# Window attention and feed-forward: probabilities turned by VectorE instead of TensorE, and the order table left out

## Chip, cores and metric

One core of a Trainium2 chip. The engines are TensorE (PE in the profile; PEld is its weight loads), VectorE (DVE), ScalarE (ACT), GpSimd (POOL) and SyncE (SP, which issues most transfers). The metric is the time of one execution in device microseconds, the median of the runs.

## What is computed

Attention of 8 batches and 8 heads (512 local and 32 global positions, 64 dimensions), then a feed-forward over the joined heads. Global queries see all keys; a local query sees the global keys and the local keys at most 32 positions away.

```python
k_all, v_all = concat([k_g, k_l]), concat([v_g, v_l])
out_g = softmax(q_g @ k_all.T / 8) @ v_all
s_ll = where(abs(pos[:, None] - pos[None, :]) <= 32, q_l @ k_l.T / 8, -1e9)
out_l = softmax(concat([q_l @ k_g.T / 8, s_ll])) @ v_all
x = concat([out_g, out_l]) with heads side by side      # (8 * 544, 512)
h = x @ w_in                                            # 512 -> 2048
out = (h - tanh(h)) @ w_out                             # 2048 -> 512
```

## The kernel before

All operands are fp32; the products of the feed-forward are made of three passes with each factor split into a high and a low part (`x_hi`, `x_lo`, `w_in_hi` and so on).

The attention works on pairs of heads, four pairs for each batch. The first two batches use the class `Pair` (pairs 0 to 7), the other six the class `WindowPair` (pairs 8 to 31, L1441). A window pair goes through these steps:

- loads of keys and queries in blocks of 32 rows (L1459), turned on VectorE in 32x32 blocks (L1472, L1475);
- scores of each block of 32 queries against its three neighbouring blocks and the global keys, 128 small matmuls into two PSUM banks (L1497), and scores of the global queries into two more (L1519);
- a softmax: mask and minimum on VectorE (L1597, L1531), exponentials on ScalarE (L1605, L1561), reciprocals on VectorE (L1611, L1612), normalisation on GpSimd (L1619, L1566). The local probabilities lie in `win_probs`, one buffer for all pairs, one half for each head;
- turning the probabilities, so that keys stand on partitions: 16 TensorE transposes with the identity into two PSUM banks (`transposes`, L1632 to L1644), and two copies into `win_kf` (`add_turned`, L1646, by the helper L998) by ScalarE or VectorE;
- the probabilities of the global queries turned by VectorE (L1586);
- values loaded (L1721), two products, one for each half of the positions (`product`, L1655, matmuls at L1677), and their results split into `x_hi` and `x_lo` (L1706, L1710) with the global part added up in `xg`.

The feed-forward of batch b-1 (class `Chunk`, L1785) runs beside the attention of batch b. It has 16 steps: a hidden step of three passes of four 512-column matmuls (L1816), tanh on ScalarE (L1824), a subtraction on VectorE (L1827) that also frees the hidden step's bank, the split into `ghi` and `glo` (L998, and L1833 on GpSimd or VectorE), and three passes of four output matmuls (L1864). The buffers of that split exist twice. Banks 0 to 3 are shared by hidden steps and the attention, banks 4 to 7 hold the output sums. The last batch's feed-forward and that of the global rows form the tail (class `Tail`, L2035).

The order of all instructions comes from a planner (class `Order`, L51), which runs while the kernel is being built. Every operation has an engine (or a choice, as in `either`, L1000, and `subtract`, L1007), a cost, a due time, what it reads, writes and waits for (`r`, `w`, `res`), and the banks that it takes and frees. The planner always takes the operation that can start first; among those that can start within 0.08 us of each other, the one with the smallest due time. Due times have units of their own: `base(i)` grows by 102.2 for each head, hidden steps are 53.6 apart, and `after(us)` of a window pair is `at` plus 8 for each us. `at` is `base(2j) + CFG["win"]`. Several operations of TensorE can be glued into a visit (`add_visit`, L1682): they run one right after the other, and the banks of all of them are taken before the first.

Before it runs, two tables change the operations by their number: `NUDGE` shifts the due time of 2979 operations (58 to 3036), `CHOICE` adds to the delay that 583 of them have on an engine (L2463 to L2470).

Two visits of a window pair j follow from this (L1976): scores with global scores of j; and products of pair j-1 with transposes of j.

Of the kernel before, what the change touches and what calls it, by code (L numbers as in the profile page):

```python
# [16 lines left out]
P = 128  # L17
# [190 lines left out]
def kernel(ctx, tc, q_l, k_l, v_l, q_g, k_g, v_g, w_in, w_out, out):  # L208
# [107 lines left out]
    def bank(shape, j, dt=F32):  # L316
# [6 lines left out]
        elif len(shape) == 4:  # L323
# [4 lines left out]
    CFG = dict(win=-300.0, a_g=0.7314, a_kg=2.7836, a_ph=2.671, a_qs=2.1456, a_w=0.2133, a_wn=0.6018, a_xg=7.3446, d_g=1.3367, d_gl=1.6793,  # L328
# [20 lines left out]
    NUDGE = {58: -82.9303, 59: -189.1326, 60: -114.5462, 61: -87.6488, 62: -87.6488, 63: -92.8616, 64: -66.6432,  # L349
# [1626 lines left out]
    def window_attention(j):  # L1976
        p, last = pairs[j], pairs[j - 1]
        first = last.b < 2
        if first:
            add_window_masks()  # L1980
        if p.jj == 0:
            add_globals(p.b)
# [527 lines left out]
```

## Time and profile before

| | us |
|---|---|
| median of 3 runs | 952.76 (952.22 to 953.66) |
| the profiled execution | 954.22 |
| its span, first to last instruction | 952.4 |
| PE busy in it | 934.4 |
| DVE, ACT, POOL busy | 550.8, 387.7, 321.7 |

The profile is of one execution. A busy time is the union of an engine's instructions, and the share is of the span. The first feed-forward matmul starts at 62.3 us, the first scores of a window pair at 190.33 us; the tail begins at about 819 us.

### The profile page before, as it was taken

The page shows a single profiled execution, that of the slowest core. Times are in us where ns is not written, and L with a number is a line of the kernel's source. Part 1 is how long each engine was busy: PE and PEld are TensorE (multiplying, and loading weights), DVE is VectorE, ACT ScalarE, POOL GpSimd, SP SyncE. Part 2 cuts the span into 40 slices and gives each one's busy share as a digit, 9 for nine tenths or more (in the row PEclk, how much of TensorE's full clock was granted, in tenths as well). Part 3 has the DMA queues.
Part 4 walks back from the last instruction along what each step waited for, and adds up shares of the span by engine and source line. Part 5 has one row for each costly group of instructions (what it writes and reads, how often), then busy time and mean ns, then how long its engine had stood idle before and what let it go on. Part 6 is the DMA issues. An engine that isn't in the chain of part 4 may idle for free.

```text
span 952.4 us, 24784 instructions
## 1 busy us (share of the span) xinstructions
PE 934.4 (98%) x9762; PEld 769.1 (81%) x9762; DVE 550.8 (58%) x1840; ACT 387.7 (41%) x1116; POOL 321.7 (34%) x637
## 2 busy tenths in 40 slices
PE   7889999999999999999999999999999999999998
PEld 5667877788888888888888878888888888899896
DVE  6977876564556464554544554454555345767773
ACT  6865656353424333433423333342233431424232
POOL 4755645642434332323423333321332331020000
PEclk9989999999999999999999999999999999999999
DMA  9655433622534343334424332242334220100001
GB/s 231 174 145 155 125 109 101 128 48 42 89 62 107 59 71 62 84 80 68 69 48 99 67 63 53 55 82 49 62 66 103 40 40 1 45 1 1 1 1 66
DMA packets 243572, 70.29 MB, mean 74 GB/s; under 512 B 228096, under 2 KB 236800, under 8 KB 243456
## 3 DMA queue, kind: packets, MB, share of 16 engines
q1 hardware_dynamic: 242112, 68.19, 33.5%
q8 instruction: 76, 1.25, 0.6%
q10 hardware_dynamic: 1344, 0.52, 0.2%
q14 instruction: 40, 0.33, 0.1%
HBM read 59.77 MB, written 8.91 MB: 72 GB/s over the span
## 4 chain that ended last, share of the span: by engine, by line
PE 94%; DMA 2%; DVE 2%; issue 1%; ACT 1%; POOL 0%; SPq 0%; ACTq 0%; POOLq 0%; DVEq 0%
PE bank L1864 33%; PE bank L1816 32%; PE bank L2191 7%; PE bank L2311 5%; PE bank L1677 5%; PE bank L1497 3%; PE bank L1641 2%; PE bank L1519 1%; PE bank L1368 1%; PE bank L2217 1%; PE bank L1271 1%; DMA first_raw<-in_k_l_dram 1%; PE bank L1291 1%; PE bank L1175 1%; DMA first_q<-in_moe_w_in_dram 1%
## 5 line engine op out<-in xcount | busy, mean ns | idle before, releaser
L1833 POOL TENSOR_TENSOR glo<-t,ghi 128x512 fp32r<-128x512 f32 x83 | 107.8, 1299 | 269.9 <-PE bank L1864 149.3
L1827 DVE TENSOR_TENSOR t<-bank,t 128x512 f32<-128x512 f32 x112 | 77.3, 691 | 189.4 <-ACT t L1824 189.3
L1824 ACT ACTIVATE t<-bank 128x512 f32<-128x512 f32 x112 | 67.0, 599 | 244.9 <-PE bank L1816 224.1
L1864 PE MATMUL bank<-w_out_hi,glo 128*128 128x512 f32 x448 | 126.6, 397 | 0.0
L1864 PE MATMUL bank<-w_out_hi,ghi 128*128 128x512 f32 x448 | 126.3, 396 | 0.0
L1864 PE MATMUL bank<-w_out_lo,ghi 128*128 128x512 f32 x448 | 125.1, 393 | 0.0
L1816 PE MATMUL bank<-x_hi,w_in_hi 128*128 128x512 f32 x448 | 121.1, 393 | 0.0
L1816 PE MATMUL bank<-x_lo,w_in_hi 128*128 128x512 f32 x448 | 120.0, 390 | 0.0
L1816 PE MATMUL bank<-x_hi,w_in_lo 128*128 128x512 f32 x448 | 119.9, 391 | 0.0
L1605 ACT ACTIVATE prob<-prob,st 128x128 f32<-128x128 f32 x192 | 74.8, 391 | 70.4 <-DVE st L1597 69.9
L1816 PEld LDWEIGHTS bank<-x_hi,w_in_hi 128*128 128x128 f32 x448 | 83.6, 189 | 18.4 <-issue 0.6
L1816 PEld LDWEIGHTS bank<-x_lo,w_in_hi 128*128 128x128 f32 x448 | 83.9, 188 | 17.9 <-issue 0.2
L1816 PEld LDWEIGHTS bank<-x_hi,w_in_lo 128*128 128x128 f32 x448 | 83.6, 188 | 18.2 <-issue 0.8
L1864 PEld LDWEIGHTS bank<-w_out_lo,ghi 128*128 128x128 f32 x448 | 83.6, 188 | 18.3 <-issue 0.5
L1864 PEld LDWEIGHTS bank<-w_out_hi,glo 128*128 128x128 f32 x448 | 83.1, 189 | 18.7 <-issue 0.7
L1864 PEld LDWEIGHTS bank<-w_out_hi,ghi 128*128 128x128 f32 x448 | 82.5, 188 | 18.7 <-issue 1.1
L1619 POOL TENSOR_SCALAR prob<-prob,st 128x128 f32<-128x128 f32 x192 | 69.4, 382 | 76.1 <-DVE st L1612 41.7
L998 ACT CAST ghi<-t 128x512 fp32r<-128x512 f32 (+1 forms) x73 | 44.4, 608 | 46.0 <-PE bank L1864 29.0
L1597 DVE CUSTOM_DVE_ANT_0 prob<-bank,wraw 128x128 f32<-128x128 f32 x192 | 44.6, 283 | 30.0 <-PE bank L1497 30.0
L998 ACT COPY keys_first<-bank 128x512 f32<-128x512 f32 (+2 forms) x83 | 37.2, 497 | 47.6 <-PE bank L1641 33.3
L1677 PEld LDWEIGHTS bank<-keys_first,values 128*64 128x64 f32 x672 | 42.1, 138 | 8.5 <-issue 5.3
L1677 PE MATMUL bank<-keys_first,values 128*64 128x32 f32 (+2 forms) x672 | 46.7, 228 | 0.0
(258 smaller groups left out, 1526.2 us busy)
## 6 DMA issues: line engine op xcount, KB each, us to landing
values<-in_v_l_dram SPq DMA_DIRECT2D x24, 336.0 KB, 4.0
keys_first<-in_v_l_dram SPq DMA_DIRECT2D x24, 336.0 KB, 5.2
out_dram<-wpair SPq DMA_DIRECT2D x28, 256.0 KB, 2.4
rawkq<-in_q_l_dram SPq DMA_DIRECT2D x96, 64.0 KB, 2.3
rawkq<-in_k_l_dram SPq DMA_DIRECT2D x96, 64.0 KB, 2.3
first_q<-in_moe_w_in_dram SPq DMA_DIRECT2D x6, 512.0 KB, 4.5
stage<-in_moe_w_out_dram SPq DMA_DIRECT2D x6, 512.0 KB, 4.4
wpair<-in_moe_w_out_dram SPq DMA_DIRECT2D x6, 512.0 KB, 4.5
```

The costliest lines, as they stand in the source:

```text
L998: (nc.scalar.copy if e == "A" else nc.vector.tensor_copy)(dst, src)
L1597: nc.vector.tensor_tensor_reduce(out=self.prob[h][:, c], in0=self.box["s"][h][:, c], in1=win_mask(t), scale=-0.125, scalar=1e30, op0=ALU.a ...
L1605: nc.scalar.activation(x, x, AF.Exp, bias=s[:, k:k + 1], scale=-1.0, accum_out=s[:, 8 + k:9 + k])
L1619: nc.gpsimd.tensor_scalar(x, x, s[:, k:k + 1], 1.0, op0=ALU.mult, op1=ALU.mult)
L1677: nc.tensor.matmul(dst, win_values[h][:, window(b)], src, start=n == 0, stop=n == len(parts) - 1, skip_group_check=True)
L1816: nc.tensor.matmul(self.h[s][:, j * n:(j + 1) * n], w[:, cc, f * P:(f + 1) * P], self.x()[xi][:, cc, :n], start=part == 0 and cc == 0 and ...
L1824: nc.scalar.activation(tt_[q], self.h[s], AF.Tanh)
L1827: nc.vector.tensor_sub(tt_[q], self.h.pop(s), tt_[q])
L1833: eng[e].tensor_sub(gg[q][1], tt_[q], f32(gg[q][0]))
L1864: nc.tensor.matmul(self.acc[tt], g[:, j * self.n + tt * P:j * self.n + (tt + 1) * P], low_out(f) if wi else high_out(f), start=s == 0 and ...
L2191: nc.tensor.matmul(self.hold(tt, tags), g(), low_out(f) if wi else high_out(f), start=first and k < len(tts), stop=last and k == len(mms) - 1)
L2311: nc.tensor.matmul(dst[:, at], w, m, start=fresh and n == 1, stop=n == 6, skip_group_check=True)
```

## The change

In the window batches the 16 TensorE transposes of a pair and the two copies out of PSUM are gone. Instead `add_turns` issues 16 turns on VectorE from `win_probs` into `win_kf`, eight operations of two instructions. Each instruction takes 32 partitions (block row i of the queries) with 2 heads x 4 tiles x 32 columns and writes 32 partitions (block k of the keys). The products wait for all of them.

The visits are cut otherwise: the global scores of pair j alone; then the products of j with the scores of pair j+1. The next pair's loads are added before that visit. The results of a product are due 18 and not 36 after `at`, and `win` goes from -300 to -100, by which everything in a window pair is due 200 units later. `NUDGE` and `CHOICE` are empty, for all operations, those of the first two batches and of the tail included.

```diff
-    CFG = dict(win=-300.0, a_g=0.7314, a_kg=2.7836, a_ph=2.671, a_qs=2.1456, a_w=0.2133, a_wn=0.6018, a_xg=7.3446, d_g=1.3367, d_gl=1.6793,
+    CFG = dict(win=-100.0, a_g=0.7314, a_kg=2.7836, a_ph=2.671, a_qs=2.1456, a_w=0.2133, a_wn=0.6018, a_xg=7.3446, d_g=1.3367, d_gl=1.6793,
...
-    NUDGE = {58: -82.9303, 59: -189.1326, 60: -114.5462, 61: -87.6488, 62: -87.6488, 63: -92.8616, 64: -66.6432,
...
-    CHOICE = {58: {"A": 7.329, "D": -0.1536}, 76: {"D": -0.24362, "A": -0.2133}, 77: {"D": -0.6068},
...
+    NUDGE = {}
+
+    CHOICE = {}
...
-        def transposes(self):
...
-                            nc.tensor.transpose(box[x][:, h, t], self.prob[h][r, t * P:t * P + P], idn[r, r])
...
-        def add_turned(self):
-            def store(x):
+        def add_turns(self):
+            def turn(k, half):
                 def fn(e, _):
-                    copy(e, view(win_kf, [(CH, 2), (P, NT), (1, 64)], 3 * G + 64 * x), self.box["t"][x])
-                return fn
-
-            for x in range(2):
-                add(either(512, "tp", True), store(x), self.after(9.0), r=[("t", self.j, x)], w=[f"h{x}"], free=[(("t", self.j, x), 1)])
+                    for i in (2 * half, 2 * half + 1):
+                        src = view(win_probs[W * i:W * i + W], [(S, 2), (P, NT), (1, W)], W * k)
+                        nc.vector.transpose(view(win_kf[W * k:W * k + W], [(CH, 2), (P, NT), (1, W)], 3 * G + W * i), src)
+                return fn
+
+            r = [self.p(h, tp) for h in range(2) for tp in range(2)]
+            for k in range(4):
+                for half in range(2):
+                    add(("D", 0.85), turn(k, half), self.after(9.0), r=r, w=[f"hb{k}{half}"], res=self.over)
...
-            return dict(fn=mm, d=0.9, names=[o], r=["h0", "h1", "hg0", "hg1", "vh"], res=[k + (0,) for k in x], rows=1.0, ldw=0.053,
+            return dict(fn=mm, d=0.9, names=[o], r=[f"hb{k}{n}" for k in range(4) for n in range(2)] + ["hg0", "hg1", "vh"], res=[k + (0,) for k in x], rows=1.0, ldw=0.053,
...
-            due = self.after(36.0)
+            due = self.after(18.0)
...
     def window_attention(j):
-        p, last = pairs[j], pairs[j - 1]
-        first = last.b < 2
-        if first:
+        p, other = pairs[j], pairs[j + 1] if j + 1 < len(pairs) else None
+        if j == H:
             add_window_masks()
-        if p.jj == 0:
             add_globals(p.b)
-        p.add_load()
-        p.add_visit(p.at, [p.scores(), p.global_scores()])
+            p.add_load()
+            p.add_visit(p.at, [p.scores()])
+        p.add_visit(p.after(1.0), [p.global_scores()])
         p.add_softmaxes()
         p.add_global_softmax()
-        p.add_visit(p.after(9.0), ([] if first else [last.product(0), last.product(1)]) + [p.transposes()])
-        if not first:
-            last.add_outputs()
-        p.add_turned()
         p.add_values()
         for h in range(2):
             p.add_global_transpose(h)
+        p.add_turns()
+        if other:
+            if other.jj == 0:
+                add_globals(other.b)
+            other.add_load()
+        p.add_visit(p.after(16.0), [p.product(0), p.product(1)] + ([other.scores()] if other else []))
+        p.add_outputs()
...
-    p = pairs[-1]
-    p.add_visit(p.after(32.0), [p.product(0), p.product(1)])
-    p.add_outputs()
```

## Rows read from the trace of the kernel before

**Rows 1.** The page's span and its busy times: us, share of the span, instructions.
```profile
span 952.4 us, 24784 instructions
...
PE 934.4 (98%) x9762; PEld 769.1 (81%) x9762; DVE 550.8 (58%) x1840; ACT 387.7 (41%) x1116; POOL 321.7 (34%) x637
```

**Rows 2.** The page's chain that ended last, by engine.
```profile
PE 94%; DMA 2%; DVE 2%; issue 1%; ACT 1%; POOL 0%; SPq 0%; ACTq 0%; POOLq 0%; DVEq 0%
```

**Rows 3.** Windows of four stages: stretch, length, busy times, PE's granted clock, DMA.
```profile
0.00:60.00 60.00, 47.95 (x485) 35.55 (x487) 46.33 (x188) 45.29 (x146) 31.86 (x65) 0.94 0.74 185
60.00:190.00 130.00, 130.00 (x822) 101.96 (x819) 93.67 (x255) 71.83 (x178) 74.21 (x112) 1.00 0.48 127
190.00:815.00 625.00, 623.27 (x7801) 513.43 (x7800) 320.17 (x1231) 222.72 (x705) 205.78 (x451) 1.00 0.34 64
815.00:952.40 137.40, 133.18 (x661) 118.22 (x659) 90.61 (x169) 47.85 (x90) 9.80 (x10) 1.00 0.05 20
```

**Rows 4.** Timeline of PE, a visit of products and transposes: start, duration, line, form.
```profile
261.01 1.07 PE L1864 MATMUL bank<-w_out_lo,ghi 128*128 128x512 f32 x4
261.92 1.07 PE L1864 MATMUL bank<-w_out_hi,glo 128*128 128x512 f32 x4
262.92 0.30 PE L1677 MATMUL bank<-keys_first,values 128*64 128x96 f32 x1
...
264.62 0.25 PE L1677 MATMUL bank<-keys_first 128*64 128x96 f32 x1
264.80 0.71 PE L1641 MATMUL bank<-idr,prob 64*128 64x64 f32 x16
265.44 1.19 PE L1816 MATMUL bank<-x_hi,w_in_hi 128*128 128x512 f32 x4
```

**Rows 5.** Line L1641, the transposes: durations, first and last start.
```profile
L1641 PE MATMUL bank<-idr,prob x384: 221/222/278, 200.5 to 779.4; 64*128 64x64 f32 x192
```

**Rows 6.** Groups by form, VectorE's turns: count, busy us, mean ns, idle before.
```profile
L1475 DVE STREAM_TRANSPOSE hi<-rawkq 128x512 f32<-128x512 f32 x24 | 16.9, 703 | 7.6 <-PE bank L1497 7.5
...
L1586 DVE STREAM_TRANSPOSE keys_first<-pg 128x192 f32<-128x192 f32 x48 | 16.2, 362 | 14.9 <-PE bank L1677 11.0 <-POOL pg L1566 3.2 <-POOL glo L1833 0.5
```

**Rows 7.** Timeline of VectorE, a turn and the instruction behind it.
```profile
195.07 0.71 DVE L1472 STREAM_TRANSPOSE first_m<-rawkq 128x512 f32<-128x512 f32 x1
195.70 0.32 DVE L1531 CUSTOM_DVE_ANT_0 pg<-bank,wraw 128x192 f32<-128x192 f32 x1
```

**Rows 8.** Groups by form, evictions into keys_first (win_kf's tile) on ScalarE.
```profile
L998 ACT COPY keys_first<-bank 128x512 f32<-128x512 f32 x61 | 33.7, 590 | 45.8 <-PE bank L1641 33.3 <-PE bank L1291 9.5 <-DVE st L1557 2.8
```

**Rows 9.** Timelines of PE and GpSimd, the first window pair.
```profile
190.33 1.43 PE L1497 MATMUL bank<-first_m,hi 64*32 64x64 f32 x124
...
195.21 1.42 POOL L1619 TENSOR_SCALAR prob<-prob,st 128x128 f32<-128x128 f32 x4 [0.41 <-DVE st L1612]
...
197.40 1.43 POOL L1619 TENSOR_SCALAR prob<-prob,st 128x128 f32<-128x128 f32 x4
```

**Rows 10.** The page's transfers: issues, KB each, median us to landing.
```profile
values<-in_v_l_dram SPq DMA_DIRECT2D x24, 336.0 KB, 4.0
keys_first<-in_v_l_dram SPq DMA_DIRECT2D x24, 336.0 KB, 5.2
```

**Rows 11.** Timeline of PE, a visit of scores and what follows it.
```profile
661.54 1.43 PE L1497 MATMUL bank<-first_m,hi 64*32 64x64 f32 x124
...
663.35 1.20 PE L1864 MATMUL bank<-w_out_hi,glo 128*128 128x512 f32 x4
...
666.21 1.07 PE L1816 MATMUL bank<-x_hi,w_in_hi 128*128 128x512 f32 x4
```

**Rows 12.** Timeline of VectorE behind that visit, first and fourth of eight.
```profile
663.06 0.29 DVE L1597 CUSTOM_DVE_ANT_0 prob<-bank,wraw 128x128 f32<-128x128 f32 x1 [1.84 <-PE bank L1497]
...
663.70 0.29 DVE L1597 CUSTOM_DVE_ANT_0 prob<-bank,wraw 128x128 f32<-128x128 f32 x1
```

**Rows 13.** Windows, a stretch of lower clock; columns as in rows 3.
```profile
47.80:54.60 6.80, 4.65 (x23) 2.58 (x25) 5.25 (x20) 4.93 (x13) 3.82 (x6) 0.50 0.54 143
```

More of the change, by code (lines that the diff above doesn't have):

```diff
@@ L1630, in add_softmaxes @@
                     add(("P", 0.77), norm(h, tp), due(3.5 + 2.0 * h), r=[("inv", self.u, h)], w=[self.p(h, tp)])
-        def transposes(self):
-            names = [("t", self.j, x) for x in range(2)]
-            def mm(e, tags):
-                box = self.box["t"] = [bank([P, 2, NT, 64], tags[n]) for n in names]
-                for h in range(2):
-                    for t in range(NT):
-                        for x in range(2):
-                            r = slice(64 * x, 64 * x + 64)
-                            nc.tensor.transpose(box[x][:, h, t], self.prob[h][r, t * P:t * P + P], idn[r, r])
-            return dict(fn=mm, d=0.57, names=names, r=[self.p(h, tp) for h in range(2) for tp in range(2)] + ["idr"], res=["h0", "h1"] + self.over,
-                        rows=0.7, ldw=0.053, tail=0.053, mode="r")
-        def add_turned(self):
-            def store(x):
+        def add_turns(self):
+            def turn(k, half):
                 def fn(e, _):
-                    copy(e, view(win_kf, [(CH, 2), (P, NT), (1, 64)], 3 * G + 64 * x), self.box["t"][x])
-                return fn
-            for x in range(2):
-                add(either(512, "tp", True), store(x), self.after(9.0), r=[("t", self.j, x)], w=[f"h{x}"], free=[(("t", self.j, x), 1)])
+                    for i in (2 * half, 2 * half + 1):
+                        src = view(win_probs[W * i:W * i + W], [(S, 2), (P, NT), (1, W)], W * k)
+                        nc.vector.transpose(view(win_kf[W * k:W * k + W], [(CH, 2), (P, NT), (1, W)], 3 * G + W * i), src)
+                return fn
+            r = [self.p(h, tp) for h in range(2) for tp in range(2)]
+            for k in range(4):
+                for half in range(2):
+                    add(("D", 0.85), turn(k, half), self.after(9.0), r=r, w=[f"hb{k}{half}"], res=self.over)
         def product(self, half):
@@ L2047, in __init__ @@
             self.acc = {}
-            self.was = ["raw", "kq", "ww", "hk0", "gm", "h0", "h1", "vh", ("gkq", 0), ("gkq", 1), "pg00", "pg01", "pg10", "pg11", "pw00", "pw01", "pw10", "pw11", "pg0", "pg1", "pl0", "pl1", "p00", "p10",
+            self.was = ["raw", "kq", "ww", "hk0", "gm", *[f"hb{k}{n}" for k in range(4) for n in range(2)], "vh", ("gkq", 0), ("gkq", 1), "pg00", "pg01", "pg10", "pg11", "pw00", "pw01", "pw10", "pw11", "pg0", "pg1", "pl0", "pl1", "p00", "p10",
                         "p01", "p11", "h00", "h01", "h10", "h11", "hg0", "hg1", "vh0", "vh1", "ga", "gb", ("wraw", 2)]
```

630 rows, old and new, of tables (CHOICE, NUDGE) are left out of this document.

## Prediction

> **What bounds the kernel now.** I read the page's head first: PE is busy 934.4 of 952.4 us, and the chain that ended last is PE for 94% [rows 1, 2]. Then the stages: PE lacks 12.0 us before 60 us, nothing from 60 to 190, 1.7 us from 190 to 815 and 4.2 us after that [rows 3]. A matmul that is merely late by a tenth would still look busy there, so I went to the timeline of PE: groups of four 512-column matmuls follow each other at 0.91 us, and the next visit of the attention begins as soon as the last has been fed in [rows 4]. So between 60 and 815 us the kernel is as long as the list of its matmuls. Two things follow. Work taken off PE there shortens the kernel by its full length. And nothing in the order can be improved there: a new order can only put idle time in, or leave it as it is.
>
> **What leaves PE.** In the window batches a pair's probabilities are turned by 16 transposes [rows 5], 24 pairs. One such set stands on PE from 264.80 us, and the next feed-forward matmul starts at 265.44 us [rows 4]: 0.64 us. A little of the switch may go too: from the last product, at 264.62 us, to the first transpose there are 0.18 us, against 0.09 us from the feed-forward (its last group is through at 261.92 + 0.91 us) to the first product at 262.92 us [rows 4]; that is at most 0.10 us more. 24 x 0.64 = **15.4 us** off the path; the bounds are 15.4 and 24 x 0.74 = 17.8 us. I take 15.4, because another kind of work (the scores) takes the place behind the products and pays a switch of its own. The visits stay two for each pair: products with the next scores, and the global scores alone, where there were scores with global scores, and products with transposes. So the number of switches between attention and feed-forward stays.
>
> **What comes to VectorE.** 16 instructions a pair of 32 partitions x 256 elements. No row has that form. The nearest are the 512-element turn at 703 ns and the 192-element one at 362 ns, both on 128 partitions [rows 6]. Elements per partition set the time in them: (703 - 362) / 320 = 1.07 ns an element, so an estimate for 256 from the two is 430 ns. Back to back, a 0.71 us turn lets the next instruction in after 0.63 us [rows 7], so in a row they cost about 0.35 us. A pair costs 16 x 0.35 = 5.6 to 16 x 0.43 = 6.9 us, 24 pairs 134 to 165 us. I take 6.2 us, 150 us in all; the price can't be below the lower bound unless a quarter of the partitions made an instruction shorter, which no row tells. VectorE is busy 320 of 625 us in that stage [rows 3]; with 150 more, 470 of 610, it is at 77% (80% at the upper bound). So by itself it doesn't become the bound, and this costs nothing while PE has other work ready; the cover is the feed-forward of the batch before.
>
> The Trainium skill's page "VectorE: DVE Perf Modes" speaks against the change: its section "Rules for kernel authors" gives a 128x128 turn to TensorE where the result may land in PSUM, and "The three transpose paths" has VectorE at 311 ns for 128x128 in bf16, in blocks of 32x32 only. An estimate by that page would be 8 x 0.311 = 2.5 us a pair on full partitions; the sum on the path would be the same by it, since either figure leaves VectorE below its limit. [...]
>
> **What goes with the transposes.** Two evictions a pair of 590 ns on ScalarE (the group holds those of the first batches too) [rows 8], some 28 us, all off the path; two of four PSUM banks in that visit; and the hand-over to them. They cost nothing now and give nothing.
>
> **The loop of a pair** gets tighter. Products, and with them the next pair's scores, now wait for the 16 turns of the same pair, where the scores used to wait only for the transposes. In the first window pair the scores start at 190.33 us and the last local normalisation ends at 198.82 us [rows 9]: 8.5 us. Add the turns, 6.2 us; what VectorE does for the feed-forward meanwhile, some 2 us at its present half load; an estimated 1.5 us (two subtractions or peaks of VectorE) until four banks are free; and 1.9 us for the products ahead of the scores: 20 us. Pairs are now (779.4 - 200.5) / 23 = 25.2 us apart [rows 5], 24.5 with the transposes gone. So there is room for 4 us a pair. Against the feed-forward the products come 52 units of due time later (at base + 28, where it was base - 24), which is one hidden step of 53.6; that costs nothing as long as the loop has this room. The turns wait for GpSimd's normalisation; queued behind them on VectorE are the feed-forward's subtractions, which free the banks of PE's next hidden step. GpSimd itself isn't slowed: four normalisations took 1.42 us beside VectorE's turn of 195.07 us and 1.43 us at 197.40 us [rows 7, 9].
>
> **Transfers.** Values are asked for at the same place of the pair (10 units after it) but wanted by the products some 18 us later and not a pair later. They land within 5.2 us of their issue [rows 10], so the softmax still hides them; without that cover it would be 4 to 5 us a pair. Behind them in SP's queue come the next pair's keys and queries, which are needed later still. Nothing.
>
> **The order table.** It gave each of nearly 3000 operations a shift of its due time and some 580 a bias to an engine. It is what makes PE gapless now, or it isn't; the trace has no run without it, so I bound it. In the window stage the weak spot is a visit: a visit with four banks leaves the hidden step without one. At 661.54 us such a visit begins, PE is back on feed-forward at 663.35 us, and VectorE has read the first head's scores at 663.99 us [rows 11, 12]. A hidden step can't start before about 664.2 us, so 0.8 us have to be covered, more when VectorE is in the middle of something else. Now three passes of output matmuls do that, until 666.21 us [rows 11]. The order decides whether they are left. Lower end: they always are, 0 us. Upper end: never, 48 visits x 0.8 = 38 us. The new pairing eases it (the products' banks come free while the scores run, the global scores take two banks), a VectorE at 77% makes it worse. I take one visit in three and 1.0 us, **16 us**: nearer to the lower end, as the steps repeat and the planner sees the banks.
>
> Before 190 us, engines are close to each other: up to 60 us VectorE works 46.3 and ScalarE 45.3 of 60, PE 48.0 [rows 3], and while PE waits its clock is down to 0.50, the 1.2 GHz level, for 6.8 us [rows 13]. There every late eviction shows. Ends: -2 us (its 12 us of idle time aren't sacred) and 12 us, as much idle time again; I take **5 us**. At the end of the kernel the operations have a sequence of their own by construction; ends 0 and 4.2 us, as much again; I take **2 us**. Together 23 us, from -2 to 54.
>
> **The sum.** The profiled execution took 954.2 us, 1.8 more than its span and 1.5 more than the median of 952.8. 954.2 - 15.4 + 23 = 961.8, in terms of the median **960.3 us**: slower by 0.8%.
>
> **The other ways.**
> - *PE stays fed* (faster). The planner finds output passes for every visit without its table; then only the first term counts, with a few us at the start and the end: 952.8 - 15.4 + 0 to 8 = 937 to 946, say 941. For it: the slack above of 4 us a pair, two banks less in one visit, and dues by which the feed-forward comes ahead of the turns. Against: PE has nothing left to gain there, so that every miss counts in full. It decides where the stalls of all stages stay under 13.5 us. 37%.
> - *They cancel* within 0.2%, 950.9 to 954.7, stalls of 13.5 to 17.3 us. That 0.2% is about what a measurement of this kernel can tell from no change. 11%.
> - *VectorE takes over* (slower still). If a turn of 32 partitions cost what a 512-element one costs, 0.70 us, a pair would pay 11.2 us: VectorE at (320 + 269) / 610 = 97%, the loop at 25 us and more, over the 24.5 us that there are. With 1 to 2 us over, 24 pairs cost 24 to 48 us on top of the forecast: 985 to 1008 us. It decides from a turn of about 0.6 us on (VectorE at 90%, a loop of 23.4 us). Against: the price by elements per partition [rows 6]. 10%.
> - The forecast: idle time spread in small pieces over the visits and the start. 42%.
>
> **Chances.** Faster 0.37, same 0.11, slower 0.42 + 0.10 = 0.52. The likeliest case alone spans 955 to 975. The range is 940 to 984: some 0.10 lie below (the transposes' upper bound and no stalls at all), 0.07 above (most of the third case).
>
> **What would show it.** Right: L1641's successor on VectorE, 384 instructions of 0.35 to 0.43 us; PE's busy time less by about 15 us; VectorE at 75 to 80% from 190 to 815 us; PE idle there 10 to 20 us, in pieces of 0.3 to 2 us before hidden matmuls, released by VectorE or ScalarE; its idle time before 60 us at 14 to 20 us. If PE's idle time from 190 to 815 us stays below 5 us, the table was worth nothing there, and the first of the other ways is right. If it is in long pieces before the first hidden step of a batch, the loop was too long, and the third is. If the turns take over 0.5 us, my price by elements per partition fails.

## The result and the profile after

| | before | after |
|---|---|---|
| median of the runs, us | 952.76 (952.22 to 953.66) | 944.01 (943.83 to 945.8), 3 runs |
| profiled execution, us | 954.22 | 943.83 |
| its span, us | 952.4 | 942.0 |
| PE idle in the span, us | 18.0 | 19.5 |

The ratio is 0.9913, with an interval of 0.9890 to 0.9935: 0.9% faster. The forecast was 0.8% slower (960.3); the first of its other ways, "PE stays fed" with 937 to 946 us, is what happened. The two profiles differ by 10.4 us.

The page of the kernel after: span, busy times, the chain by engine, and the group of the new turns (busy us and mean ns; then VectorE's idle time before them).

```profile
span 942.0 us, 24357 instructions
...
PE 922.5 (98%) x9387; PEld 754.8 (80%) x9387; DVE 702.5 (75%) x2281; ACT 367.2 (39%) x1075; POOL 342.8 (36%) x573
...
PE 91%; DVE 3%; ACT 2%; issue 1%; POOL 1%; DMA 1%; ACTq 0%; POOLq 0%; SPq 0%; DVEq 0%
...
L1007 DVE STREAM_TRANSPOSE keys_first<-prob 32x256 f32<-32x256 f32 x384 | 167.3, 436 | 10.3 <-POOL prob L989 4.0
```

PE is still the bound, with 11.9 us less busy time [rows 1] and 1.5 us more idle time (942.0 - 922.5 against 952.4 - 934.4). So the gain lies in PE's busy time, and little of it was given back in idle time. VectorE took 151.7 us more without getting in the way. The turns are 167.3 us of its time; other work left it, since the planner now gives all 112 subtractions that make `glo` to GpSimd, where 29 of them were on VectorE before.

The stages of the kernel after, as in [rows 3]: busy time (and instructions) of PE, PEld, DVE, ACT, POOL, then the granted clock, the DMA share and GB/s.

```profile
0.00:60.00 60.00, 51.05 (x523) 38.41 (x524) 48.82 (x195) 46.59 (x151) 35.46 (x67) 1.00 0.74 185
60.00:190.00 130.00, 128.86 (x943) 99.40 (x942) 81.80 (x242) 81.16 (x207) 80.66 (x123) 1.00 0.47 125
190.00:805.00 615.00, 609.80 (x7264) 499.13 (x7265) 477.55 (x1676) 190.16 (x627) 217.54 (x377) 1.00 0.34 65
805.00:942.00 137.00, 132.80 (x659) 117.91 (x657) 94.33 (x171) 49.33 (x93) 9.15 (x8) 1.00 0.06 20
```

PE lacks 8.95 us before 60 us (12.0 before), 1.14 from 60 to 190 (0), 5.2 in the window stage (1.7), 4.2 at the end (4.2). The start got 3 us better without the table, and the clock of the first stage is 1.00: the stretch at 0.50 [rows 13] is gone. The 5.2 us of the window stage are put down by the waits of PE, from 60 to 805 us (us in total, times, longest; three more of 0.3 us each, all before 190 us, are left out):

```profile
PE bank L867 <- issue: 4.5, 5, 1.2
PE bank L889 <- DVE first_m L842: 1.0, 1, 1.0
...
```

No wait of the window stage is one for a turn of the probabilities, a bank, an eviction or a value. The second line is the second pair's global scores, at 190.65 us, for that pair's keys, which VectorE had still to turn. The first one stands inside the scores, where "issue" says that PE waited for no engine or operand that the profile names (more in experiment 5). Two visits in the timeline of PE show it:

```profile
204.25 1.07 PE L1224 MATMUL bank<-w_out_hi,glo 128*128 128x512 f32 x4
205.25 0.30 PE L1037 MATMUL bank<-keys_first,values 128*64 128x96 f32 x1
...
207.13 1.66 PE L867 MATMUL bank<-first_m,hi 64*32 64x64 f32 x123
209.99 0.31 PE L867 MATMUL bank<-first_m,hi 64*32 64x64 f32 x5 [1.20 <-issue]
210.22 0.50 PE L1176 MATMUL bank<-x_hi,w_in_hi 128*128 128x512 f32 x1
...
231.11 0.30 PE L1037 MATMUL bank<-keys_first,values 128*64 128x96 f32 x1
...
232.99 1.49 PE L867 MATMUL bank<-first_m,hi 64*32 64x64 f32 x128
234.40 1.20 PE L1176 MATMUL bank<-x_hi,w_in_hi 128*128 128x512 f32 x4
```

The visit at 231.11 us is whole: products and 128 scores in 3.29 us, 3.39 with the switch from the feed-forward. In the one at 205.25 us PE stops after 123 scores, with five to go. The kernel before has one such pause, in its global scores:

```profile
571.79 0.32 PE L1519 MATMUL bank<-first_m,win_gq 64*32 64x64 f32 x9 [1.73 <-issue]
...
574.49 1.91 PE L1864 MATMUL bank<-w_out_hi,glo 128*128 128x512 f32 x4
```

The visits of a pair, taken from the trace (median, us, each with its switch in):

```
before  scores + global scores 1.90    products + transposes 2.61    sum 4.51
after   global scores          0.58    products + scores     3.39    sum 3.97
```

So a pair gained 0.54 us, 24 pairs 13.0 us. The pauses in the scores, by the starts of the matmuls around them, add some 5.6 us to five visits of after and 1.9 us to one of before: 3.7 us more. The wait at 190 us costs 1.1 us, and the matmuls of the first two batches' attention, with the waits between them, take 2.6 us less than before. -13.0 + 3.7 + 1.1 - 2.6 = -10.8, for 10.4 us between the profiles. The sum leaves out smaller shifts in the feed-forward. One of them is in before: from 573.43 us, right behind its pause, the granted clock was 0.50 (the 1.2 GHz level) for 3.4 us, and the group at 574.49 us above takes 1.71 us to the next one's start instead of 0.91.

### The profile page after: what moved, and what is told of

It reads as the page before. It is cut to its first block, busy times and chain, and to the rows that moved or that the text cites. A ratio compares the mean times of both kernels' runs of the same rounds, so it can differ in the third digit from the quotient of the medians.

```text
span 942.0 us, 24357 instructions
## 1 busy us (share of the span) xinstructions
PE 922.5 (98%) x9387; PEld 754.8 (80%) x9387; DVE 702.5 (75%) x2281; ACT 367.2 (39%) x1075; POOL 342.8 (36%) x573
## 4 chain that ended last, share of the span: by engine, by line
PE 91%; DVE 3%; ACT 2%; issue 1%; POOL 1%; DMA 1%; ACTq 0%; POOLq 0%; SPq 0%; DVEq 0%
PE bank L1224 33%; PE bank L1176 32%; PE bank L1550 7%; PE bank L1670 5%; PE bank L1037 5%; PE bank L867 4%; PE bank L889 1%; PE bank L641 1%; PE bank L1576 1%; PE bank L738 1%; DMA first_raw<-in_k_l_dram 1%; PE bank L545 1%; POOL wraw L779 0%; DMA first_raw<-in_q_l_dram 0%; PE bank L661 0%
## 5 line engine op out<-in xcount | busy, mean ns | idle before, releaser
L1193 POOL TENSOR_TENSOR glo<-t,ghi 128x512 fp32r<-128x512 f32 x112 | 145.7, 1301 | 286.0 <-PE bank L1224 192.8
L1007 DVE STREAM_TRANSPOSE keys_first<-prob 32x256 f32<-32x256 f32 x384 | 167.3, 436 | 10.3 <-POOL prob L989 4.0
L1224 PEld LDWEIGHTS bank<-w_out_hi,ghi 128*128 128x128 f32 x448 | 82.5, 188 | 20.7 <-ACT wpair L368 1.2
L1037 PE MATMUL bank<-keys_first 128*64 128x32 f32 (+2 forms) x672 | 46.7, 228 | 0.0
```

The costliest lines, as they stand in the source:

```text
L1007: nc.vector.transpose(view(win_kf[W * k:W * k + W], [(CH, 2), (P, NT), (1, W)], 3 * G + W * i), src)
L1037: nc.tensor.matmul(dst, win_values[h][:, window(b)], src, start=n == 0, stop=n == len(parts) - 1, skip_group_check=True)
L1193: eng[e].tensor_sub(gg[q][1], tt_[q], f32(gg[q][0]))
L1224: nc.tensor.matmul(self.acc[tt], g[:, j * self.n + tt * P:j * self.n + (tt + 1) * P], low_out(f) if wi else high_out(f), start=s == 0 and ...
```

## Experiments

Two theories at first. A: the order table is worth little, and what counts is the work taken off PE. B: the table is worth some 20 us, and something else that came with the change (the new pairing of visits, the due times) pays it back. No run changes the due times by themselves. Each ratio is against the kernel before on the same chip, whose median was 953.7 to 954.2 us.

**1. The kernel before without its table.**

```diff
-    NUDGE = {58: -82.9303, ...
+    NUDGE = {}
-    CHOICE = {58: {"A": 7.329, ...
+    CHOICE = {}
```

> The kernel before with both tables empty and nothing else changed: 16 TensorE transposes a pair stay. Theory A (the table is worth nothing, the planner alone keeps PE fed): 949 to 957 us, PE idle under 6 us between 190 and 815 us, and the first feed-forward matmul as early as in the changed kernel, 58 to 60 us. Theory B (the table was worth what I had forecast, and only the new cut of the visits makes it needless): 962 to 985 us, with PE idle in short pieces behind the visits that take four banks.

Measured: 955.41 us, ratio 1.0019 (1.0006 to 1.0031). Its stages, in the columns and the windows of [rows 3]:

```profile
0.00:60.00 60.00, 50.99 (x522) 38.37 (x522) 48.81 (x194) 46.13 (x149) 34.79 (x66) 1.00 0.72 179
60.00:190.00 130.00, 128.88 (x945) 100.03 (x945) 79.31 (x223) 80.11 (x199) 81.53 (x122) 1.00 0.48 129
190.00:815.00 625.00, 622.43 (x7655) 513.52 (x7655) 336.61 (x1361) 222.11 (x696) 207.09 (x334) 1.00 0.34 64
815.00:952.40 137.40, 131.49 (x652) 116.52 (x650) 91.56 (x166) 46.97 (x87) 9.21 (x8) 0.99 0.06 20
```

PE idles 3.0 us less before 60 us, and 1.1, 0.9 and 1.3 us more in the other three stages (its span ends at 952.0 us, 0.4 us ahead of the last window). Theory A holds: by the medians (955.41 against 954.24) the table is worth 1.2 us, by the ratio 1.8 (0.6 to 3.0), where I had put 23, and without it PE is nearly as gapless in the window stage as with it (2.6 us idle of 625, against 1.7). The first feed-forward matmul starts at 59.1 us, 62.3 with the table. The kernel after has no table either and a ratio of 0.9913: between the two, the turns, the pairing and the due times are worth some 10 to 11 us.

**2. The old table's entries for the first two batches, in the kernel after** (those of operations added ahead of the first window pair).

```diff
-    NUDGE = {}
+    NUDGE = {58: -82.9303, ...
-    CHOICE = {}
+    CHOICE = {58: {"A": 7.329, ...
...
+    NUDGE = {i: x for i, x in NUDGE.items() if i < first_window[0]}
+    CHOICE = {i: x for i, x in CHOICE.items() if i < first_window[0]}
```

> The changed kernel with the old table's entries for the operations that exist unchanged in both kernels, those added before the first window pair (first two batches, weights, first feed-forward). If the table was worth my 5 us at the start: 937 to 941 us. If the planner alone is as good or better there (the first hidden step came at 58.5 us without it and at 62.3 us with it): 944 to 949 us, with the first hidden step at 61 to 63 us again.

Measured: 951.76 us, ratio 0.9974 (0.9964 to 0.9983), some 6 to 8 us slower than after (by the ratios, and by the medians). The first and the third of its stages:

```profile
0.00:60.00 60.00, 48.72 (x479) 36.26 (x481) 45.91 (x188) 45.07 (x146) 31.92 (x65) 0.94 0.74 185
...
190.00:805.00 615.00, 604.76 (x7271) 494.72 (x7251) 475.30 (x1660) 190.97 (x631) 218.98 (x393) 1.00 0.33 65
```

The clock is down again in the first stage, and the first feed-forward matmul starts at 62.5 us as in before; in after it starts at 58.5. That is 4 us. The window stage, for which no entry was put back, idles 10.2 us instead of 5.2: 6.2 us of that are pauses on "issue" (4.5 in after), the rest waits for VectorE. So this part of the table was a loss at the start. In the kernel before, the rest of it earned that back: in experiment 1 the stages from 60 us on idle 3.3 us more without it.

**3. The kernel after once more, unaltered**, as the measure for the runs that follow.

> The changed kernel unaltered, on the chip of the next three, so that they can be compared with it: 0.991 of the kernel before, as it was (944.0 to 952.8 us).

Measured: 944.55 us, ratio 0.9901 (0.9886 to 0.9916).

**4. The 16 transposes put back on PE, beside the turns** (their results are not used). In the first kernel eight stand ahead of each product, those of one half of the partitions together. The products' planned time grows with them.

```diff
+                turned, r = bank([P, 2, NT, 64], tags[o]), slice(64 * half, 64 * half + 64)
+                for h in range(2):
+                    for x in range(NT):
+                        nc.tensor.transpose(turned[:, h, x], self.prob[h][r, x * P:x * P + P], idn[r, r])
...
```

> The changed kernel with the 16 transposes put back on TensorE ahead of the products, eight for each product, written into the products' own banks and overwritten by them; VectorE's turns stay and are what is used. If the transposes' time on PE is what the change saves, 24 x 0.64 = 15.4 us come back: 957 to 962 us. If the gain came from elsewhere (an earlier start, a shorter tail), it is 944 to 950 us. A longer run of short instructions may add up to 3 us of waits inside the scores.

Measured: 980.14 us, ratio 1.0271 (1.0254 to 1.0288), twice what I expected. Then all 16 ahead of the first product, the halves of the partitions taking turns, as the kernel before has them:

> As the earlier kernel with the transposes put back on TensorE, but in the old form: ahead of the first product, all 16, upper and lower half of the partitions in turn, into the two products' banks, overwritten by them; VectorE's turns stay and are what is used. In the earlier one the transposes of one half stood together, and the trace has them 0.080 us apart instead of 0.040. In turn they should cost 0.64 us a pair again: 24 x 0.64 = 15.4 us more than the changed kernel, 13 to 19 with the fetch's waits in the longer visit. If the pairing in turn is not what doubled them, it is 30 us or more again.

Measured: 966.16 us, ratio 1.0132 (1.0113 to 1.0150). One set of each in PE's timeline, the first kernel's and the second's, with the matmul that follows:

```profile
205.32 0.71 PE L1034 MATMUL bank<-idr,prob 64*128 64x64 f32 x8
205.96 0.30 PE L1041 MATMUL bank<-keys_first,values 128*64 128x96 f32 x1
```

```profile
231.27 0.71 PE L1037 MATMUL bank<-idr,prob 64*128 64x64 f32 x16
231.91 0.30 PE L1044 MATMUL bank<-keys_first,values 128*64 128x96 f32 x1
```

Eight transposes of one half take 0.64 us, and so do sixteen that alternate: 0.080 against 0.040 us each. In the first kernel they cost 24 x 1.28 = 30.7 of the 35.6 us that it takes over experiment 3. In the second they cost 24 x 0.64 = 15.4 us of PE's time, the term of my sum; of the other 6 us of the 21.6 that it takes over experiment 3, 3.4 are more pauses within the scores and 2.9 more at output steps. So work put on PE comes back in the time at its full length, and the longer visits cost some more. The row of its pauses (waits of PE):

```profile
PE bank L867 <- issue: 7.1, 10, 1.6
```

**5. Are the pauses in the scores those of PE's instruction supply?** Counted from the start of the program, weight loads, matmuls and PE's waits on semaphores alike, the five pauses of after come ahead of PE's instructions 3522, 5314, 9666, 14018 and 15298. Each of these numbers leaves 194 when divided by 256; so does the one pause of before. So 16 instructions were taken out far ahead of the window stage (eight matmuls that only fill PE's time there):

```diff
+        if less[0] and n > 2:
+            less[0] -= 1
+            n -= 1
```

> The changed kernel with eight of 93 idle-time matmuls (line 1832, before 60 us) left out, which moves everything behind them 16 instructions forward in PE's stream and changes no order. The five waits inside the scores all stand where the instruction's number is 194 modulo 256, and only in visits where that number falls on the visit's last 60 of 368 instructions (at 325, 353, 353, 359 and 363); where it falls on 297 or earlier there is none. If it is the fetch of 256 instructions, the waits go to other visits, and by that pattern one of a middle size stays (at 341, the visit of pair 25), two may show a trace of it (311 and 313): 5.6 us become 1 to 1.5 us, and the kernel is 4 us faster than the unaltered one, 0.9955 of it. If the waits belong to what those visits need, they stay at the same visits, and the time is within 1 us of the unaltered one.

Measured: 945.78 us, ratio 0.9912 (0.9896 to 0.9928), the same as after. The pauses went to other places of the visits, five in the scores and three behind them (waits of PE):

```profile
PE bank L867 <- issue: 3.6, 5, 0.9
PE bank L1224 <- issue: 2.2, 3, 1.0
```

Each still falls at 194 of 256, four of them at the very counts of after (5314, 9666, 14018 and 15298), which are now 16 instructions further on in the work. That settles that they go by the count of PE's instructions and not by what the instructions do or wait for. That they could be steered out of the visits, as I had guessed, was wrong.

How many there are rises with the length of the run of short matmuls. In instructions of one visit: at most 256 (experiments 6 and 7), no wait of PE above 0.15 us within the scores; 320 (before, and experiment 1), 1 visit of 24; 368 (after, and experiment 9), 5 and 7 of 23; 400 (the second kernel of experiment 4), 10 of 23. The pace counts too: the first kernel of experiment 4 has 400 as well, with its transposes at half the pace, and its scores pause in 5 visits of 23.

The traces also show what PE waits for. The profile has 73 transfers of the kind "instruction" on queue 8 in after, for 18873 instructions of PE, and 76 in before for 19651, so one for each full 256:

```profile
q8 instruction: 73, 1.20, 0.6%
...
q8 instruction: 76, 1.25, 0.6%
```

Each is 16384 bytes. Number k of them, counted from the first, always lands ahead of PE's instruction 256 k + 194: in none of the twelve traces does that instruction start less than 1.2 us after the landing, and the five pauses of after end 1.3 to 1.6 us after it.

**6. Visits cut shorter: the scores alone first, products with global scores behind them.**

```diff
-        p.add_visit(p.after(1.0), [p.global_scores()])
+            p.add_visit(p.after(1.0), [p.global_scores()])
...
-        p.add_visit(p.after(16.0), [p.product(0), p.product(1)] + ([other.scores()] if other else []))
+        if other:
+            p.add_visit(p.after(16.0), [other.scores()])
+        p.add_visit(p.after(16.5), [p.product(0), p.product(1)] + ([other.global_scores()] if other else []))
```

> The changed kernel with the visits cut otherwise: scores of the next pair alone, then the products with the next pair's global scores; all the work is the same. Five visits of products with scores lost 0.6 to 1.4 us each in the middle of the scores, each at the same instruction number modulo 256 of PE's stream. If that is PE running out of fetched instructions in a run of 368 short ones, runs of at most 256 and 176 lose less: 5.6 us of waits go to 0 to 2, and the visits themselves take 1.51 + 2.35 instead of 3.97 us a pair: 936 to 941 us. If those waits are for something else that the scores need, they stay: 942 to 947 us.

Measured: 963.2 us, ratio 1.0098 (1.0076 to 1.0120), outside both expectations. The pauses are gone, and other waits have come (waits of PE):

```profile
PE bank L867 <- DVE first_m L842: 12.0, 11, 2.5
PE bank L1224 <- DVE ghi L368: 4.9, 1, 4.9
```

Now the scores stand ahead of the products, and PE waits for VectorE to turn the next pair's keys (L842).

**7. The same cut with the products first.**

```diff
...
+        p.add_visit(p.after(16.0), [p.product(0), p.product(1)] + ([other.global_scores()] if other else []))
+        if other:
+            p.add_visit(p.after(16.1), [other.scores()])
```

> The kernel after with its pair of visits paired the other way: products with the global scores of the next pair first, the local scores of the next pair alone behind them, so that no visit has more than 256 matmuls in a row. All work is kept. If what the earlier splitting lost (963 us) came from scores that were asked for before their operands were there, the operands now have the products in front of them, the pauses inside the scores (5.6 us in five visits) go, and the time is 939 to 942 us. If the order or the additional switch (24 x 0.1 to 0.2 us) costs more than the pauses, it is 945 us or more.

Measured: 956.7 us, ratio 1.0027 (1.0016 to 1.0037). The time is that of the second expectation; the cause is a wait. One row of PE's waits, and what VectorE did in the longest of them (VectorE's timeline):

```profile
PE bank L1224 <- DVE ghi L368: 7.8, 2, 4.9
```

```profile
295.94 0.64 DVE L956 STREAM_TRANSPOSE keys_first<-pg 128x192 f32<-128x192 f32 x2
296.60 3.60 DVE L1007 STREAM_TRANSPOSE keys_first<-prob 32x256 f32<-32x256 f32 x8
300.21 1.29 DVE L1187 TENSOR_TENSOR t<-bank,t 128x512 f32<-128x512 f32 x2
301.41 0.41 DVE L368 CAST ghi<-t 128x512 fp32r<-128x512 f32 x1
```

Eight turns of a pair stand ahead of the feed-forward's subtraction and of the cast that PE's next output step needs. This is the queue on VectorE of which the prediction spoke. In the kernel after, the 16 turns of a pair even stand in one unbroken row for 13 of the 24 pairs, and there PE has other work meanwhile; here it had none ready.

**8. VectorE loaded more: 24 turns a pair** (eight of them done twice, into the same place).

```diff
+                    nc.vector.transpose(view(win_kf[W * k:W * k + W], [(CH, 2), (P, NT), (1, W)], 3 * G + W * i), src)
...
-                    add(("D", 0.85), turn(k, half), self.after(9.0), r=r, w=[f"hb{k}{half}"], res=self.over)
+                    add(("D", 1.27), turn(k, half), self.after(9.0), r=r, w=[f"hb{k}{half}"], res=self.over)
```

> The changed kernel with 24 instead of 16 turns a pair (every second one issued twice). VectorE, 477.6 us busy of 615 between 190 and 805, goes to 561, 91%; the loop of a pair from about 22 to 25.5 us. If PE's other work still covers it (VectorE isn't near the bound): within 3 us of the changed kernel. If the loop or VectorE is close to deciding, as my third case had it from turns of 0.6 us on: 10 to 35 us more than the changed kernel, with PE idle ahead of the first hidden steps of a batch.

Measured: 971.82 us, ratio 1.0182 (1.0164 to 1.0201), 27 us over experiment 3. Its window stage and the waits of PE that lead:

```profile
190.00:805.00 615.00, 594.62 (x6936) 483.04 (x6935) 539.36 (x1756) 190.82 (x612) 208.95 (x377) 0.99 0.33 64
...
PE bank L1177 <- DVE xg L1075: 7.1, 5, 3.4
PE bank L1038 <- DVE keys_first L1008: 5.4, 6, 1.9
PE bank L1225 <- DVE ghi L368: 3.4, 1, 3.4
```

84 us more of turns on VectorE, of which 27 came out at the end. VectorE is busy 539.36 of 615 us there, 88%. PE idles 15.5 us more than in experiment 3 (36.2 us against 20.7 in the span), in waits for VectorE: the five of the first line stand ahead of hidden steps. In such waits or right behind them begin three stretches, 17.1 us together, in which the granted clock was 0.50; PE was busy for 15.9 us of them, so an estimate of what the lower clock cost is half of that, 8 us.

**9. VectorE loaded less: eight turns a pair** (from the second window pair on every second turn is left out, so half of the turned probabilities are those of the first pair).

```diff
-                    for i in (2 * half, 2 * half + 1):
+                    for i in (2 * half, 2 * half + 1)[:2 if self.j == H else 1]:
...
-                    add(("D", 0.85), turn(k, half), self.after(9.0), r=r, w=[f"hb{k}{half}"], res=self.over)
+                    add(("D", 0.85 if self.j == H else 0.43), turn(k, half), self.after(9.0), r=r, w=[f"hb{k}{half}"], res=self.over)
```

> The kernel after with every second turn on VectorE left out from the second window pair on (so half of the turned probabilities are those of the first pair): 8 instead of 16 a pair, 23 x 8 x 0.436 = 80 us less on VectorE, the same matmuls on TensorE. It asks whether VectorE's load costs the kernel after anything. If at 78% it is all covered, as my prediction had it, the time stays at 944 us within 2 us. If the load already costs what is missing of the first rival's sum, it comes out at 940 us or lower, with fewer waits of the scores and of the hidden steps.

Measured: 948.72 us, ratio 0.9948 (0.9932 to 0.9965), outside both expectations. Its window stage, and the waits of PE there:

```profile
190.00:805.00 615.00, 607.74 (x7249) 496.43 (x7250) 409.21 (x1519) 182.12 (x609) 216.09 (x366) 1.00 0.33 65
...
PE bank L867 <- issue: 4.2, 7, 0.9
PE bank L1037 <- DVE keys_first L1007: 0.8, 1, 0.8
PE bank L1176 <- DVE xg L1074: 0.7, 1, 0.7
```

80 us of turns less on VectorE (68 us less in all in this stage, since the planner gave it other work) bring nothing; the time is even some 4 us longer than after's (0.9948 against 0.9901). With other costs the planner puts the work in another order, and PE meets two waits that after doesn't have, 1.5 us; what the rest comes from isn't traced. So at 78% VectorE's load costs nothing that this run can tell, while at 88% it does. The run also shows that an order by itself is worth a few us: that much of a difference between these kernels, the 1.2 us of experiment 1 among them, should not be put down to the one thing that was edited.

## Why the prediction was wrong

- **What bounds it**: right. PE 98% busy, the chain PE for 91%, and work added to PE came back in the time at its full length (experiment 4).
- **The transposes**: 15.4 us, right as the price of the transposes (experiment 4: 0.64 us a pair). As the gain of the change it was 2.4 us too large. I argued that the number of visits stays, so that the switches cancel; but the visits got 0.54 us a pair shorter and not 0.64, so that 0.10 us a pair went back to the new cut.
- **The turns**: 436 ns each, where I had 350 to 430 and took the middle, by the overlap seen in [rows 7]; in a row of 16 there is none (7.22 us, 0.45 us each). 167 us in all, not 150. That VectorE came out at 477.55 / 615 = 78%, for the 77% that I had, is partly luck: the planner moved other work off it. "By itself doesn't become the bound" holds (experiment 9). The third case, from VectorE at about 90% on, fits experiment 8: at 88% it cost 1.1 us a pair. Where between 78% and 88% it begins, no run shows. What I cited of the Trainium skill's page "VectorE: DVE Perf Modes" ("Rules for kernel authors") gives a 128x128 turn to TensorE where the result may land in PSUM, and a 32x32 one within a bank to VectorE. The rule doesn't ask which engine is the bound, and here that decided. TensorE turned a pair in 0.64 us and VectorE in 7.0, but TensorE's turns cost the kernel 15.4 us and VectorE's nothing that a run shows.
- **The loop of a pair, evictions, transfers**: right in that they cost nothing; no wait of PE in the window stage of after is for a turn of the probabilities, a bank or a value. The loop is at most 21.7 us, the shortest time between two pairs' products, for the 20 that I had.
- **The order table**: this is the step that failed. I took 23 us between bounds of -2 and 54; experiment 1 measured 1 to 2, and PE's idle time grew by 1.5 us from before to after. The largest part of it, "one visit in three and 1.0 us, 16 us", had no row: in [rows 11] the output passes did cover the evictions, and I supposed that this was the table's doing. It was the planner's, whose model of banks and engines does the same without the table. PE's idle time in the window stage was not in front of hidden steps at all: at 5.2 us it is just over the 5 us that I had named as a sign, but 4.5 of it are the pauses, which the table has nothing to do with. Before 190 us I expected 5 us more idle time and it became 2 us less (3.1 less up to 60 us, 1.1 more behind it): the lower end of my own bound, with the remark that its 12 us "aren't sacred", was the true side. At the end, 2 us were expected and none came (4.2 us before and after).
- **What no step had**: the pauses at a fixed count of PE's instructions, 3.7 us more. [Rows 4] show PE's matmuls one after another, and I took that for what any order of them would give. The 1.7 us that PE lacked in the window stage of before [rows 3] were one such pause already, and I didn't ask what they were.

With the measured terms, the sum is 954.2 - 13.0 + 3.7 + 1.1 - 2.6 = 943.4 for the profiled execution, which took 943.8. The sign hung on the table alone: with 1 us in its place the prediction's sum for the profiled execution is 954.2 - 15.4 + 1 = 939.8, or 938.3 in terms of the median, within the range of "PE stays fed". It lies 5.7 us below the 944.0 measured, mostly for the new cut (2.4) and the pauses (3.7).

None of the kernels tried was faster than after.

## What to carry to other kernels

Where PE is busy without a gap, count its work: a part that is taken off it shortens the kernel by its length, less what the new order of the rest costs (here 15.4 us went and 10.4 were gained), as long as the engine that gets the work stays well under its limit; here 78% was free and 88% cost 27 us. Don't price an ordering aid by what its absence could do at worst: first ask which row shows that the aid, and not the scheduler under it, does the covering, and without such a row keep the lower bound as likely as the rest. Where short matmuls are glued into longer runs, look for "issue" waits of PE inside the run.

## What the runs showed of the hardware

- PE pauses at a fixed place of its instruction count, every time 194 of 256, when a run of short matmuls is long: none above 0.15 us at 256 instructions a visit, 1 of 24 visits at 320, 5 to 7 of 23 at 368 (0.58 to 1.42 us each in after), 10 of 23 at 400, and 5 of 23 at 400 with slower transposes. There is one "instruction" transfer of 16384 bytes on queue 8 for each 256 of PE's instructions (73 for 18873), most take 0.9 to 1.6 us, and the paused instruction starts 1.3 to 1.6 us after its transfer has landed (experiment 5). By the traces the pause is the wait for that transfer; no run changed the transfer itself.
- Transposes of 64 partitions by 128 columns follow each other after 0.040 us when the halves of the partitions alternate, and after 0.080 us when they don't (experiment 4).
- In experiment 7 the granted clock was 0.50, the 1.2 GHz level, from 301.97 to 307.23 us, behind a wait in which PE had been idle for 4.93 us; three groups of four matmuls took 5.26 us there where they take 2.7 at full clock. The same level shows around waits in experiment 8 and, for 3.4 us, behind the pause of 1.73 us in before, but not behind the pause of 1.9 us in experiment 1. So a wait of PE can cost more than its length. The row of the stretch in experiment 7 (columns as above):

```profile
301.97:307.23 5.26, 5.26 (x12) 4.10 (x13) 3.14 (x21) 3.29 (x17) 4.82 (x9) 0.50 0.30 48
```
